# Keys and queries of the first three tiles loaded and transposed by 128 tokens, and the first masks added by TensorE

## The chip, the cores and the metric

The kernel runs on one core of one Trainium2 chip. The metric is device time in microseconds (us) of one execution, the median of several runs. The engines of a core work at the same time, each through its own queue in program order: TensorE (PE, with its weight loads shown apart as PEld), VectorE (DVE), ScalarE (ACT), GpSimd (POOL) and SyncE (SP). They wait for each other through semaphores. POOL, SP and ACT also issue DMA transfers.

## What is computed

Sliding-window attention with a window of 32 tokens to each side, over 8 batches and 8 heads of 576 tokens of 64 values, followed by a two-layer network with a sigmoid-approximated GELU over all 4,608 tokens:

```python
scores = scale * np.matmul(q, k.transpose(0, 1, 3, 2))
mask = np.abs(pos[:, None] - pos[None, :]) <= window     # 32
scores = np.where(mask, scores, -1000000000.0)
attn = softmax(scores)
x = concat_heads(np.matmul(attn, v))                     # 4608 x 512
h = x @ w_in                                             # 512 x 2048
out = (h * (1.0 / (1.0 + np.exp(-1.702 * h)))) @ w_out   # 2048 x 512
```

## The kernel before

All tokens are one row of 4,608, shifted by 32 so that a unit of 128 queries needs 192 keys: three chunks of 64. There are 36 units (u), nine tiles of 512 tokens (i or T, four units each), and halves of a tile of 256 tokens (t). The order of the work on every engine is written out by hand: the program's order is the order of each queue. `head` holds the first part (units 0 to 6 of attention, the two layers of units 0 to 3, and the first layer of units 4 to 7), `pairs` the next, and then `step` runs once for each T from 3 to 10.

The attention of a unit goes through these functions. `scores(u)` makes 24 matmuls, keys as weights and queries moving, into a pair of PSUM banks of the kind "d" (there are two such pairs), and ScalarE takes the exponential into `p`. `band(u)` multiplies `p` by a 0/1 mask on VectorE, in two halves or in one. `values(u)` makes 32 matmuls of `p` with the values and a column of ones: `ve` holds 128 tokens of v, `vo` the same shifted by 64 tokens, made by `odd_v` with two copies on VectorE or POOL. `norm(u)` divides on VectorE (a reciprocal and a product, or two of each), and `x_T(u)` transposes the result for the first layer, by TensorE and a copy, or by a DMA transpose on SP.

`layer1(t, d)` is a first-layer group: eight matmuls and a GELU on ScalarE. Each half tile has eight of them; d names a part of 256 columns of w_in. `layer2(u, part)` is a piece of two matmuls of the second layer; `run(n)` in `head` issues 2n of these. From tile 2 on the two layers use sums of quarter blocks (`first_layer`, `second_layer`, `x_sums`, `g_sums`). `keep_busy(n)` issues n matmuls on a tile of zeros.

Keys lie transposed in `kT` (two heads of 64 on the partitions), a ring of 1,024 tokens; queries in `qT`, two tiles. For tiles 0 to 2 `load_heads` (L144) loads several heads of a whole tile with four neighbouring tokens on a partition, so that a packet is 4 x 64 values. `heads_T` (L206) transposes them on TensorE, one head and every fourth token at a time (64 rows to a transpose), eight for each pair of heads; VectorE copies the keys to `kT`, putting the four token classes back in order, and ScalarE copies the queries as they are. Scores of units under 12 therefore have their query columns permuted, and the exponential writes `p` in order again (L269 to L271). The first pair of heads of tile 0 comes as float32 over SP (`load_first`) and is rounded by `pair_heads`, with four full transposes. The last 64 keys that unit 3 needs come apart (`load_edge`, `edge_T`). From tile 3 on keys and queries are loaded by 128 tokens of all heads (`load_keys`, `load_queries`), a packet being 64 values, and transposed by DMA (`keys_X`, `queries_X`) or by TensorE in four full transposes (`keys_PE`, L169).

All bfloat16 and float16 loads are issued by POOL, whose queue also holds the mask's making (`setup_mask`, `cut_mask`) and some of the `odd_v` copies. A POOL load waits for the one eight before it.

Of the kernel before, what the change touches and what calls it, by code (L numbers as in the profile page):

```python
# [22 lines left out]
SQ = 64  # L23
# [10 lines left out]
class _Kernel:  # L34

    def __init__(self, ctx, tc, q, k, v, w_in, w_out, out):
# [18 lines left out]
        self.stage, self.paired = {}, set()  # L55
# [51 lines left out]
    def setup_mask(self):  # L107

        pool, m = self.nc.gpsimd, self.mask
        lo, hi = slice(0, 64), slice(64, 128)  # L110
        pool.memset(m, 1.0)
        for blks, rows, sign in ((slice(0, 2), lo, 1), (slice(0, 2), hi, -1), (slice(2, 4), lo, -1), (slice(2, 4), hi, 1)):
            ap = m[rows, blks, :]
            pool.affine_select(out=ap, in_=ap, compare_op=ALU.is_ge, fill=0.0, base=0,
                               pattern=[[0, 2], [-sign, SQ]], channel_multiplier=sign)

    def cut_mask(self):
        lo, hi = slice(0, 64), slice(64, 128)
        for b, rows, cols in ((0, hi, slice(0, 32)), (0, lo, slice(32, 64)), (2, lo, slice(0, 32)), (2, hi, slice(32, 64))):
            self.nc.gpsimd.memset(self.mask[rows, b, cols], 0.0)  # L120
# [5 lines left out]
    def load_w_in(self, c):  # L126
        w = self.DFF // 4
        self.nc.gpsimd.dma_start(self.w_in_sb[:, :, c * w:(c + 1) * w],
                                 self.w_in[:, c * w:(c + 1) * w].rearrange("(k p) f -> p k f", p=128))
# [14 lines left out]
    def load_heads(self, i, c, heads=None):  # L144

        key = (c, i)
        if key not in self.stage:
            tag, bufs = ("qs", 2) if c == "q" else (("gs3", "gs1", "gs2")[i], 1)
            self.stage[key] = self.work.tile([128, self.H, JT * self.D], BF16, name=c + "s", tag=tag, bufs=bufs)
        lo, hi = heads or (0, self.H)  # L150
        src = {"q": self.q, "k": self.k}[c]
        for off, b, s, m in self.pieces(512 * i + (32 if c == "q" else 0), 512):
            self.nc.gpsimd.dma_start(self.stage[key][off // JT:(off + m) // JT, lo:hi, :],
                                     src[b, lo:hi, s:s + m, :].rearrange("h (p j) d -> p h (j d)", j=JT))
# [51 lines left out]
    def heads_T(self, c, i, hps, kind, eng):  # L206

        tp = self.bank(kind, [128, len(hps), JT, 128], BF16, "tp")
        for a, hp in enumerate(hps):
            for j in range(JT):  # L210
                if (c, i, hp) in self.paired:
                    self.nc.tensor.transpose(tp[:, a, j, :], self.stage[c, i, "c"][:, hp, j], self.ident)
                    continue
                for t in range(2):
                    self.nc.tensor.transpose(tp[64 * t:64 * t + 64, a, j, :],  # L215
                                             self.stage[c, i][:, 2 * hp + t, j * self.D:(j + 1) * self.D], self.ident)
        to = slice(hps[0], hps[-1] + 1)
        if c == "q":
            self.cast(eng, self.qT[:, to, i % 2], tp)
            return  # L220
        at = 512 * i % RING
        self.cast(eng, self.kT[:, to, at:at + 512].rearrange("r a (p j) -> r a p j", j=JT), tp.rearrange("r a j p -> r a p j"))

    def load_first(self, c, hp):

        raw = self.stage[c, "raw"] = self.work.tile([128, 2, JT * self.D], F32, name=c + "_raw", tag="s", bufs=3)
        src = {"q": self.q, "k": self.k}[c]
        s0 = 32 if c == "q" else 0
        self.nc.sync.dma_start(raw, src[0, 2 * hp:2 * hp + 2, s0:s0 + 512, :].rearrange("h (p j) d -> p h (j d)", j=JT))

    def pair_heads(self, c, i, hp, eng, src):

        st = self.stage[c, i, "c"] = self.work.tile([128, 1, JT, 2, self.D], BF16, name=c + "c", tag="x", bufs=5)
        self.paired.add((c, i, hp))
        self.cast(eng, st[:, hp], src.rearrange("p h (j d) -> p j h d", j=JT))

    def load_edge(self):

        self.stage["edge"] = self.work.tile([64, self.H, self.D], BF16, name="edge", tag="x", bufs=5)
        self.nc.gpsimd.dma_start(self.stage["edge"], self.k[0, :, 512:576, :].rearrange("h s d -> s h d"))  # L240

    def edge_T(self, kind, eng):
        nc = self.nc
        src = self.stage["edge"]
        tp = self.bank(kind, [128, 4, 64], BF16, "tp")
        for hp in range(4):
            nc.tensor.transpose(tp[:, hp, :], src[:, 2 * hp:2 * hp + 2, :], self.ident[:64, :64])
        self.cast(eng, self.kT[:, :, 512:576], tp)

    def scores(self, u):  # L250
        nc = self.nc
        both, two = self.double("sc")
        sc = [t.rearrange("p (b s) -> p b s", s=SQ) for t in two]
        if u < 12:
            qT = self.qT[:, :, u // 4 % 2].rearrange("r h j (b s) -> r h b j s", s=16)
            b0 = u % 4 * 2
        else:
            qT, b0 = self.qT[:, :, u // 4 % 2, u % 4].rearrange("r h (b s) -> r h b s", s=SQ), 0
        for hp in range(4):
            for chunk in range(3):  # L260
                lo, blks = 64 * (chunk % 2), slice(max(chunk - 1, 0), min(chunk, 1) + 1)
                at = 64 * (2 * u + chunk) % RING
                for eo in range(2):
                    r = slice(eo * 64, eo * 64 + 64)
                    nc.tensor.matmul(sc[eo][lo:lo + 64, 2 * hp + blks.start:2 * hp + blks.stop, :], self.kT[r, hp, at:at + 64],  # L265
                                     qT[r, hp, b0 + blks.start:b0 + blks.stop],
                                     start=hp == 0 and chunk < 2, stop=hp == 3 and chunk > 0)
        p = self.work.tile([128, 2, 8, SQ], BF16, name="p", tag="p", bufs=4)
        if u < 12:  # L269
            nc.scalar.activation(p.rearrange("p e b (r j) -> p (e b) r j", j=JT),  # L270
                                 both.rearrange("p e (b j r) -> p (e b) r j", j=JT, r=16), AF.Exp, scale=self.scale)  # L271
        else:
            nc.scalar.activation(p.rearrange("p e b s -> p e (b s)"), both, AF.Exp, scale=self.scale)  # L273
# [313 lines left out]
    def keep_busy(self, n):  # L587

        junk = self.bank("d", [128, 256], F32, "junk")
        for _ in range(n):  # L590
            self.nc.tensor.matmul(junk, self.idle[:, 0:128], self.idle, start=True, stop=True)  # L591


    def head(self):

        nc, dve, act, pool = self.nc, self.nc.vector, self.nc.scalar, self.nc.gpsimd
        for c in "kq":
            self.load_first(c, 0)
        self.setup()
        for h in ((2, 4), (4, 8)):  # L600
            for c in "kq":
                self.load_heads(0, c, h)
# [4 lines left out]
        self.load_edge()  # L607
        self.load_v(3)
        self.load_v(4, 0)
        self.load_w_in(0)  # L610
        self.odd_v(1, pool)
        self.load_w_in(1)
        self.load_w_in(2)
        self.odd_v(2, pool)
        self.odd_v(3, pool)
        self.load_w_in(3)
        self.cut_mask()
        for c in range(2):
            self.load_w_out(c)
        for c in "kq":  # L620
            self.load_heads(1, c)
        self.load_w_out(2)
        self.load_v(4, 1)
        for m in range(5, 8):
            self.load_v(m)
        self.load_w_out(3)
        for c in "kq":
# [324 lines left out]
```

## Time and profile before

| What | Value |
|---|---|
| median of 3 runs | 293.45 us (292.95 to 293.47) |
| profiled execution, whole | 292.87 us |
| its span, first instruction to last | 291.2 us |
| busy PE | 279.8 us, 96% |
| busy DVE, ACT, POOL | 69%, 69%, 43% |
| HBM read, written | 36.83 MB, 9.44 MB |
| packets under 512 bytes | 126,288 of 141,687 |

A row of the page's second part cuts the span into 40 equal slices of 7.3 us and gives a busy share in tenths. Tables by stretches give busy microseconds of each engine in a stretch, with the number of instructions in brackets. The chain of waits follows the work that ended last back from the last instruction: each step is the piece of work that released the next. In the rows of DMA queues, q0 is POOL's, q1 is SP's; a share over 100% means that several packets of an engine were under way at once. Matmul ends are modelled, so a busy TensorE is not one at its peak.

The page's groups that the change touches (line, engine, operation, shapes, count; busy us, mean ns):

| Group | Count | Busy us | Mean ns |
|---|---|---|---|
| L215 PE transposes of keys, 64 rows | 88 | 3.6 | 222 |
| L215 PE transposes of queries, 64 rows | 88 | 3.5 | 220 |
| L174 PE transposes of keys, 128 rows | 32 | 3.1 | 219 |
| L270 ACT exponential, units under 12 | 12 | 11.7 | 1,025 |
| L273 ACT exponential, other units | 24 | 23.3 | 1,031 |
| L286 DVE band, half | 14 | 5.3 | 420 by halves of 128x512 |
| L124 DVE copy of keys, 128x1024 from 64-row transposes | 4 | 4.9 | 1,224 |
| L124 ACT copy of queries, 128x1024 | 4 | 4.0 | 1,012 |
| L591 PE junk matmuls | 48 | 8.4 | 310 |

A matmul's own time includes the way through the array; neighbours follow each other faster than that.

### The profile page before, as it was taken

Reading aid. Unit: us, or ns where it says so; the run is one execution under the profiler, and the core shown is the slowest. Engines: PE = TensorE matmul, PEld = TensorE weight load, DVE = VectorE, ACT = ScalarE, POOL = GpSimd, SP = SyncE. Lnnn points to the kernel's source line nnn. Section 1 sums busy time; section 2 is a strip of 40 time slices with the busy share of each in tenths; the row PEclk is TensorE's granted clock in tenths of the full one; section 3 lists DMA queues with packets and bytes.
Section 4 is the critical chain, followed back from the end, with each engine's and each line's share of the span. In section 5 each row is a group of like instructions: output and inputs, shape, how many; then the busy total and the mean of one; then the engine's idle time right before and its main releaser. Section 6 shows DMA issues by size and latency. Waiting matters only on the chain.

```text
span 291.2 us, 8833 instructions
## 1 busy us (share of the span) xinstructions
PE 279.8 (96%) x3692; PEld 224.5 (77%) x3692; DVE 200.8 (69%) x404; ACT 201.6 (69%) x301; POOL 125.5 (43%) x191
## 2 busy tenths in 40 slices
PE   6789999999999999999899999999999999999995
PEld 4558855776866768888788888888888788888884
DVE  3467346887467579777867787778777877737752
ACT  3475625589795679768966897689758975756830
POOL 8894465839983398539326926802100000000000
PEclk9999999999999999999999999999999999999999
DMA  7999999999999999999999999999703120300223
GB/s 133 162 206 202 192 184 181 220 131 146 155 142 150 111 175 119 150 139 118 155 168 123 146 198 136 154 145 181 80 2 144 24 56 0 147 0 2 79 104 108
DMA packets 141687, 37.60 MB, mean 129 GB/s; under 512 B 126288, under 2 KB 137552, under 8 KB 141648
## 3 DMA queue, kind: packets, MB, share of 16 engines
q0 software_dynamic: 98528, 18.16, 86.2%
q1 hardware_dynamic: 41040, 15.35, 34.9%
q10 hardware_dynamic: 2080, 3.54, 4.8%
q8 instruction: 29, 0.48, 0.7%
q14 instruction: 10, 0.08, 0.1%
HBM read 36.83 MB, written 9.44 MB: 159 GB/s over the span
## 4 chain that ended last, share of the span: by engine, by line
PE 75%; ACT 15%; DVE 3%; issue 2%; DMA 2%; POOL 1%; POOLq 0%; ACTq 0%
PE h_ps L432 28%; PE o_ps L503 21%; PE h_ps L343 10%; PE o_ps L355 8%; ACT p L273 6%; PE pv L302 3%; ACT g L438 3%; ACT L273 2%; DMA ks<-in_k_dram 2%; PE tp L215 2%; ACT L585 2%; PE sc L265 1%; ACT h_ps L449 1%; DVE p L286 1%; PE junk L591 1%
## 5 line engine op out<-in xcount | busy, mean ns | idle before, releaser
L432 PEld LDWEIGHTS <-w_in_s 128*128 128x128 f16 x448 | 42.7, 97 | 10.7 <-issue 3.6
L438 ACT ACTIVATE g<-h_ps 128x512 f16<-128x512 f32 x49 | 29.2, 595 | 28.3 <-PE h_ps L432 26.6
L503 PEld LDWEIGHTS <-g 128*128 128x128 f16 x448 | 43.4, 98 | 5.2
L432 PEld LDWEIGHTS <-w_in_sb 128*128 128x128 f16 x336 | 32.5, 98 | 7.4 <-issue 0.6
L193 POOL DMA_DIRECT2D ve<-in_v_dram x40 | 33.7, 859 | 7.1 <-DMA w_out_sb<-in_moe_w_out_dram 4.0
L183 POOL DMA_DIRECT2D qu<-in_q_dram x30 | 24.1, 809 | 29.5 <-DMA qT<-qu 20.7
L503 PEld LDWEIGHTS <-gs 128*128 128x128 f16 x336 | 32.8, 98 | 4.2
L467 DVE TENSOR_TENSOR c<-h_ps,c 128x512 f32<-128x512 f32 x28 | 19.2, 687 | 22.3 <-PE h_ps L432 19.4
L203 POOL COPY vo<-ve 64x264 int32<-64x264 int32 x57 | 27.1, 475 | 17.1 <-DMA ve<-in_v_dram 9.4
L438 ACT ACTIVATE g<-c 128x1024 f16<-128x1024 f32 (+1 forms) x35 | 34.0, 970 | 0.0
L432 PE MATMUL h_ps<-xT,w_in_s 128*128 128x256 f16 x224 | 33.6, 272 | 0.0
L432 PE MATMUL h_ps<-xs,w_in_s 128*128 128x256 f16 x224 | 31.7, 272 | 1.4 <-issue 0.9
L432 PE MATMUL h_ps<-xT,w_in_sb 128*128 128x256 f16 x224 | 32.4, 272 | 0.3
L355 PE MATMUL o_ps<-w_out_sb,g 128*128 128x512 f16 x128 | 32.6, 380 | 0.0
L161 POOL DMA_DIRECT2D ks<-in_k_dram x27 | 22.8, 853 | 20.3 <-PE tp L174 9.7
L503 PE MATMUL o_ps<-w_out_s,g 128*128 128x256 f16 x224 | 31.5, 273 | 0.0
L343 PE MATMUL h_ps<-xT,w_in_sb 128*128 128x256 f16 x256 | 30.5, 273 | 0.0
L503 PE MATMUL o_ps<-w_out_s,gs 128*128 128x256 f16 x224 | 29.5, 272 | 0.0
L286 DVE TENSOR_TENSOR p<-p,mask 128x1024 bf16<-128x1024 bf16 (+1 forms) x43 | 24.8, 599 | 5.5 <-ACT p L270 3.3
L343 PEld LDWEIGHTS <-w_in_sb 128*128 128x128 f16 x256 | 24.2, 98 | 3.3 <-DVE xT L124 0.2
L503 PE MATMUL o_ps<-w_out_sb,g 128*128 128x256 f16 x224 | 26.6, 273 | 0.0
L345 ACT ACTIVATE g<-h_ps 128x512 f16<-128x512 f32 x32 | 18.9, 596 | 9.2 <-PE h_ps L343 9.1
(91 smaller groups left out, 468.7 us busy)
## 6 DMA issues: line engine op xcount, KB each, us to landing
ve<-in_v_dram POOLq DMA_DIRECT2D x32, 128.0 KB, 7.6
out_dram<-o_sb SPq DMA_DIRECT2D x6, 512.0 KB, 4.9
out_dram<-o_sb ACTq DMA_DIRECT2D x6, 512.0 KB, 6.8
ks<-in_k_dram POOLq DMA_DIRECT2D x23, 128.0 KB, 9.1
qu<-in_q_dram POOLq DMA_DIRECT2D x18, 128.0 KB, 8.9
out_dram<-o_sb SPq DMA_DIRECT2D x9, 256.0 KB, 4.6
w_in_sb<-in_moe_w_in_dram POOLq DMA_DIRECT2D x4, 512.0 KB, 7.4
w_out_sb<-in_moe_w_out_dram POOLq DMA_DIRECT2D x4, 512.0 KB, 11.3
```

What stands on the lines that cost most here:

```text
L161: self.nc.gpsimd.dma_start(ks[off:off + n], self.k[b, :, s:s + n, :].rearrange("h s d -> s h d"))
L183: self.nc.gpsimd.dma_start(qu[off:off + n], self.q[b, :, s:s + n, :].rearrange("h s d -> s h d"))
L193: self.nc.gpsimd.dma_start(self.ve[m % NV][off:off + n, :, :self.D], self.v[b, :, s:s + n, :].rearrange("h s d -> s h d"))
L203: eng.tensor_copy(to, src)
L273: nc.scalar.activation(p.rearrange("p e b s -> p e (b s)"), both, AF.Exp, scale=self.scale)
L286: self.nc.vector.tensor_mul(part, part, msk.to_broadcast([128, n, 2, SQ]))
L343: nc.tensor.matmul(hps[:, i, :], self.w_in_sb[:, kr, ff * 128:(ff + 1) * 128], xT[:, kr, :], start=(i == 0 and kr == 0), stop=(i == 1 and ...
L355: nc.tensor.matmul(o_ps, g[:, ff, s * 128:(s + 1) * 128], self.w_out_sb[:, ff, :], start=(ff == 0), stop=(ff == self.NFF - 1))
L432: nc.tensor.matmul(ps[:, i, :], a[:, kr, (2 * j + i) * 128:(2 * j + i + 1) * 128], x[:, kr, :], start=first and i == 0 and kr == 0, stop=i ...
L438: act.activation(out, src, AF.Gelu_apprx_sigmoid)
L467: dve.tensor_add(c22, ps, c22)
L503: nc.tensor.matmul(out, a[:, kb, p * 128:p * 128 + 128], b[:, kb, :], start=first and n in (0, 2 * two) and kb == 0, stop=n in (3, 3 - 2 * ...
```

## The change

Tiles 0 to 2 of keys and queries are loaded by `load_units` with 128 tokens of all eight heads on the partitions, a packet being 64 values, and `units_T` transposes them in four full transposes for each unit; `both_T` does two units of keys and queries in one pair of banks. `load_raw` brings the first unit of keys and all four units of queries of tile 0 as float32 over SP and ACT, and `round_raw` rounds them. The special case of units under 12 goes.

For units 0 to 3, `scores` first adds a negative mask (-30,000 outside the window) to both banks with two matmuls by the identity, so that the exponential gives zeros there, and `band` is not called. `negative_mask` makes it on VectorE. `setup_mask` makes only the two outer mask blocks, and `cut_mask` copies them.

The order in `head` is new: w_in is loaded in two eighths and three quarters, among the loads of v; `odd_v(1)` goes from POOL to VectorE; the table of the GELU is loaded before the first `layer1`; first-layer groups come in another order; seven rounds of the second layer come before the transposes of tile 1 instead of four. In `pairs`, `odd_v` of 10, 11 and 13 goes from POOL to VectorE.

```diff
+    def negative_mask(self):
+        self.neg = self.work.tile([128, 4, 2, SQ], BF16, name="neg", tag="x", bufs=5)
+        msk = self.mask[:, 1:4:2, :].rearrange("p (o b) s -> p o b s", o=1)
+        self.nc.vector.tensor_scalar(self.neg, msk.to_broadcast([128, 4, 2, SQ]), -1.0, 30000.0, op0=ALU.add, op1=ALU.mult)
...
+    def load_units(self, c, i, units, half=None):
...
+                    self.nc.gpsimd.dma_start(self.stage[c, i][off:off + m, u], src[b, :, s:s + m, :].rearrange("h s d -> s h d"))
...
+    def both_T(self, i, units, engs):
+        tp = self.bank("d", [128, 2, 2, 4, 128], BF16, "tp")
...
+    def transpose_units(self, c, i, units, tp, n=128):
+        for a, u in enumerate(units):
+            for hp in range(4):
+                self.nc.tensor.transpose(tp[:, a, hp, :], self.stage[c, i][:n, u, 2 * hp:2 * hp + 2, :], self.ident[:n, :n])
...
+    def load_raw(self, c, u, queue):
+        raw = self.stage[c, "raw", u] = self.work.tile([128, self.H, self.D], F32, name=c + "_raw", tag="s", bufs=3)
...
+        queue.dma_start(raw, src[0, :, s0:s0 + 128, :].rearrange("h s d -> s h d"))
...
-    def scores(self, u):
+    def scores(self, u, neg=None):
...
+        for eo in range(2 if neg is not None else 0):
+            nc.tensor.matmul(two[eo], self.ident, neg.rearrange("p h b s -> p (h b s)"), start=True, stop=False)
...
     def head(self):
...
+        self.load_raw("k", 0, nc.sync)
+        self.load_raw("q", 0, act)
+        self.load_units("q", 0, ())
+        self.load_units("k", 0, (1,))
+        self.load_raw("q", 1, nc.sync)
         self.setup()
+        self.load_units("k", 0, (2,))
         for m in range(2):
             self.load_v(m)
         self.setup_mask()
         self.load_v(2)
+        self.load_units("k", 0, (3,))
+        self.load_units("k", 1, (0,), 0)
+        self.load_w_in(0, 1)
         self.load_v(3)
+        self.load_w_in(1, 2)
         self.load_v(4, 0)
+        self.load_w_in(2, 4)
         self.odd_v(2, pool)
+        self.load_w_in(4, 6)
         self.odd_v(3, pool)
+        self.load_w_in(6, 8)
...
+        self.scores(0, self.neg)
+        self.units_T("k", 0, (2,), "o", dve)
         self.odd_v(0, dve)
+        self.round_raw("q", 3, dve)
+        self.keep_busy(4, "t")
+        self.scores(1, self.neg)
+        self.keep_busy(2, "h")
+        self.values(0, "ot")
+        self.odd_v(1, dve)
         self.norm(0)
+        self.units_T("q", 0, (2, 3), "d", act)
+        self.units_T("k", 0, (3,), "d", dve)
+        self.keep_busy(2, "h")
+        self.values(1, "hh")
         self.norm(1)
+        self.keep_busy(2, "o")
+        self.x_T(0, "o", act)
+        self.keep_busy(2, "t")
+        self.scores(2, self.neg)
+        self.units_T("k", 1, (0,), "t", dve, 64)
+        self.x_T(1, "h", dve)
+        self.keep_busy(4, "h")
+        self.scores(3, self.neg)
+        self.gelu_table()
         self.layer1(0, 0)
         self.values(2)
         self.norm(2)
         self.values(3)
         self.norm(3)
+        self.layer1(0, 1)
         self.x_T(2, "t")
         self.x_T(3, "o")
+        self.layer1(1, 0)
+        self.layer1(1, 1)
...
-        run(4)
+        run(7)
+        self.both_T(1, (0, 1), (dve, act))
+        run(1)
+        self.both_T(1, (2, 3), (dve, act))
...
+        self.load_v(8)
+        self.load_keys(3, (0,))
+        for m in (9, 10, 11, 12):
+            self.load_v(m)
         self.load_queries(3)
+        self.load_keys(3, (1, 2, 3))
...
     def pairs(self):
...
-        self.odd_v(10, pool)
...
         self.norm(8)
+        self.odd_v(10, dve)
         self.x_T(8)
...
-        self.odd_v(11, pool)
...
         self.band(10, 1)
+        self.odd_v(11, dve)
...
         self.x_T(11)
+        self.odd_v(13, dve)
```

## The prediction

> **What bounds the kernel now.** I read the page's busy rows first, then the busy time by stretches, then the chain of waits, then the opening's timeline.
>
> ```profile
> span 291.2 us, 8833 instructions
> PE   6789999999999999999899999999999999999995
> DMA  7999999999999999999999999999703120300223
> 0.00:24.00 24.00, 18.87 (x312) 13.12 (x313) 11.82 (x41) 12.17 (x16) 20.91 (x42) 1.00 1.30 170
> 24.00:64.00 40.00, 40.00 (x519) 28.19 (x520) 25.77 (x49) 22.39 (x31) 21.08 (x27) 1.00 1.70 190
> 64.00:92.00 28.00, 27.05 (x510) 18.94 (x500) 19.95 (x44) 22.88 (x33) 21.50 (x30) 1.00 1.89 144
> 92.00:291.00 199.00, 193.92 (x2373) 164.30 (x2371) 143.27 (x271) 144.17 (x224) 62.04 (x93) 1.00 1.09 110
> ```
>
> In the stretches the columns are the stretch, its length, busy PE, PEld, DVE, ACT and POOL, then granted clock, DMA share and GB/s. TensorE is idle for 5.1 us before 24, for nothing between 24 and 64, and for 1.0 between 64 and 92. So this change, which ends with the third tile, can gain in two ways only: the steady TensorE stream starts earlier, or TensorE gets less to do after it has started. The junk matmuls of L591 (8.4 us in all) count as busy in the first row, so the opening holds more air than 5.1 us.
>
> ```profile
> 3.07 5.78 DMA ks<-in_k_dram
> 8.89 0.64 PE tp L215 x16
> ...
> 10.78 1.08 ACT qT L124 x2
> 12.21 1.03 ACT p L270
> ...
> 22.14 0.98 PE h_ps L343 x8
> ...
> 24.45 10.48 PE h_ps L343 x96
> 34.92 3.45 PE o_ps L355 x16
> 38.38 1.01 PE tp L215 x32
> ```
>
> The chain (start, length, what) begins with the load of heads 4 to 7 of the keys, goes through their transposes to the first exponential at 12.21, and reaches the steady stream with the third first-layer group at about 22.1. All sixteen groups are done at 34.92. That is my milestone. A steady group costs 10.48/12 = 0.873 us.
>
> **The opening, step by step.** The old order needs all 512 tokens before any score; the new one needs 128 tokens of keys and queries, then 64 more keys. What comes late in the new order is the loads, so they are counted first.
>
> ```profile
> q1 hardware_dynamic: 479, 0.47, 90.6%
> q0 software_dynamic: 1245, 0.61, 112.8%
> q0 software_dynamic: 2973, 0.39, 237.2%
> q1 hardware_dynamic: 496, 0.13, 86.6%
> q0 software_dynamic: 437, 0.05, 85.9%
> ```
>
> These are the DMA rows (packets, MB, share of 16 engines) of four windows: 2.0 to 3.7, 4.0 to 8.5, 9.5 to 12.0, and 70.3 to 71.3 us (the last two lines). Packets of 1,024, 512 and 128 bytes flow at 282, 277 and 1,189 a us; the mix of 256-byte transposes and 128-byte rows at 933. Every load of 128 tokens is now 1,024 such short packets. In the new queue order ten of them come up to the third load of v: five float32 ones on the SP and ACT queues and five on POOL's. Ten times 1,024 take 8.6 us at 1,189 and 11.0 at 933. No row shows float32 packets of 256 bytes from DRAM; I take 1,090 (9.4 us), nearer the fast end, because the slow mix holds transposes, which these loads are not. First packets flow at 1.95 us, and landing follows the last packet by about 1.05 (the second v load's packets end near 11.1, its copy starts at 12.22). So the third v load lands at 12.4, bounds 11.6 and 14.0; in the old order it lands at 12.97.
>
> Everything before it fits: first keys at about 4.4, cast 0.56, four transposes 0.4, copy 0.42 (ACT's 0.59 for the queries, which ACT rounds in 0.62), first exponential near 8.5 instead of 12.21. The negative mask (one DVE instruction on 128x512, between 0.2 and 0.7 by the DVE rows of that size) stands between two key copies that wait for loads, so I put it at nothing; uncovered it costs those 0.2 to 0.7.
>
> From 12.4 on VectorE works in a row, in program order: `odd_v(1)` two copies of 0.29 (13.0); `norm(0)` two reciprocals of 0.17 and two products of 0.42 (14.2); copy of the keys' fourth unit 0.42 (14.6); `norm(1)` 1.2 (15.8). TensorE then does x_T(1) 0.22, four junk 0.44, and the scores of unit 3: two mask matmuls of 512 columns at 0.22 (L355's rate, 3.45/16) and 0.44 as before: 17.3. Exponential 1.03 (18.4), `values(3)` 0.4. The four `band` products, eight times 0.42 with the mask, are gone from this path. VectorE's `norm(2)` and `norm(3)`, 0.9 each, run from 18.55 to 20.35; copies of x for units 2 and 3, 0.42 each: 21.2. With 0.1 us of hand-overs layer1(1,0) starts at 21.3 to 21.4, two groups being done, as at 22.08 before. Fourteen groups of 0.873 are 12.2: **33.6 against 34.92, so -1.3 us**; bounds from the landing alone -2.1 and +0.3.
>
> POOL's part: `odd_v(2)` and `odd_v(3)` stay on it (two copies of about 0.42 each), and behind them the issue of the next w_in parts (0.76 each). v unit 3 now waits behind one w_in eighth, the half unit behind two. An eighth (512 packets of 512 bytes) takes 1.3 us at the rate of the window from 44 to 46 us (790 packets in 2 us), 1.9 at the opening's 277 a us. So they land near 15.9 and 17.7, `vo` of unit 3 is ready near 18.8, when `values(3)` is issued. That is without slack: a microsecond later there is a microsecond later at the milestone.
>
> The later key and query loads, 8 times 128 tokens for each of tiles 1 and 2, grow too: 2.1 MB at 154 instead of 190 GB/s, 13.6 instead of 11.0 us. Tile 1's second half then lands near 39.5 and is transposed at 41; tile 2's lands near 52 (before 50.15) and is used from 56. Cover 1.5 and 4 us, cost nothing; if the cover went, the excess of 2.6 would show.
>
> The Trainium skill's page "DMA: Bandwidth & Descriptors" (Specifications) gives 512 bytes as the smallest transfer for line rate. By that rule the change makes the wrong choice on every key and query load, and the trace agrees in direction, 154 against 190 GB/s. The rule alone gives no time; the sum above charges what the rows show.
>
> **TensorE after the opening.** Tiles 1 and 2: 64 matmul transposes of 64 rows each, 1.01 per 32 (chain), become 32 each of 128 rows; L174's and L332's fours follow each other in 0.22, so 16 cost 0.88. Four times (1.01 - 0.88) = **-0.5**. The layer-2 calls are only reordered, scores have the same count of matmuls, and the exponential without the rearranged write costs the same (1,025 against 1,031 ns).
>
> **The stage after (64 to 92).** `odd_v(10)` and `odd_v(11)` move from POOL to VectorE, before `band(10)` and before `band(11)`, two copies of 0.39 each. VectorE has little room there: `norm(9)` would end at 75.8 instead of 74.56, and `values(11)`, which reuses its bank pair at 75.03, waits 0.75. `odd_v(13)` falls into VectorE's idle 4.92 us before 81.38 and costs nothing. Bounds 0 (hidden by earlier loads or idle moments) and 1.5 (all of it); I take **+0.6**. POOL's relief buys nothing TensorE waits for.
>
> **Sum.** -1.3 - 0.5 + 0.6 = -1.2. The profiled execution took 292.87 us (span 291.2), so 291.67; the runs' median is 293.45, 0.58 above it, so **292.2**.
>
> **Rivals.**
> *More of the same*: short packets flow at 1,189 from the start, v lands at 11.6 (-0.8 more), and VectorE's added copies hide (-0.6): -2.6, 290.85. For: 1,189 is reached as soon as 128-byte packets start. Against: the queue share there is 237%, with several loads in flight, and TensorE's fixed order has little slack.
> *Given back*: v's half unit lands a microsecond later behind the eighths at 277 packets a us, so the milestone gains 0.3 to 0.4, and the added copies cost 0.9: about 0, 293.45.
> *Slower*: the float32 loads are the bound. In the window 65.75 to 66.15, where 256-byte packets ran alone, 234 passed in 0.4 us, 585 a us: a raw load is 1.75 us, five are 8.75, and with the POOL loads behind them v lands at 16.0; at the mixed 933 it lands at 14.0. The middle, 15.0, is 2.6 later than I took: +1.4, 294.85. It decides from a landing of 13.6 on. For: no float32 load with so short packets is in the trace, and five of ten loads are such. Against: those 585 were transposes.
> The skill's page "DMA: Bandwidth & Descriptors" (Issuing engines are not separate DMA queues) says that issuing on several engines saves only issue time. By it the raw loads on SP and ACT would take engine time from v, as in this rival; nothing in this trace shows two hardware queues at once at the start.
>
> **How the numbers follow.** Forecast 0.46, more 0.22, given back 0.12, slower 0.20. About 0.2% (0.6 us) is what a measurement of this kernel can tell. The forecast's own spread, half of the way to the bounds of the landing and of the copies together, is 291.5 to 293.4, so some 0.08 of its 0.46 is within 0.2%; faster is 0.38 + 0.22 = 0.60, same 0.08 + 0.12 = 0.20, slower 0.20. The range runs from 290.4 (beyond the second case) to 295.0 (the slower one's middle).
>
> **What would show it.** First exponential near 8.5; third v load at 12.4; layer1(1,0) at 21.4 and all sixteen groups at 33.6; transposes of tiles 1 and 2 in fours of 0.22 without waits for loads; a gap of up to 0.75 before `values(11)`. A first-layer stream that waits on `ks` or `ve` loads later than 13.6 would make the forecast wrong, and so would TensorE gaps between 34 and 64, where there were none.

## The result, and the profile after

The changed kernel takes 295.08 us (median of 4 runs, 294.73 to 295.46), against 293.29 of the kernel before (4 runs, 292.95 to 293.47). The ratio is 1.0063, with an interval of [1.0045, 1.008]: it is slower, by 0.6%, where a gain, to 292.2, was forecast. The profiled execution took 295.05, its span is 293.3.

The head of the page of the changed kernel, TensorE's and the DMA engines' rows in 40 slices:

```profile
span 293.3 us, 8654 instructions
...
PE   7888999898999999999999999999999999999995
...
DMA  9999999999999999999999999982303050300133
```

TensorE is fuller in the first two slices (78 for 67) than it was, but now has an 8 in the fourth, eighth and tenth, where it had nines. The busy time by stretches, with the columns of the same table before:

```profile
0.00:24.00 24.00, 19.43 (x278) 13.02 (x281) 11.26 (x43) 11.73 (x15) 19.18 (x39) 1.00 1.49 182
24.00:64.00 40.00, 39.19 (x426) 28.06 (x424) 22.56 (x44) 21.93 (x31) 30.92 (x38) 1.00 2.00 184
64.00:92.00 28.00, 25.94 (x494) 18.19 (x493) 20.12 (x47) 23.42 (x33) 17.46 (x23) 1.00 2.34 145
```

TensorE's idle time was 0 between 24 and 64 and is 0.81; between 64 and 92 it was 0.95 and is 2.06. Who is waited for is in the table of TensorE's waits from 24 to 92 us (total, times, longest):

```profile
PE pv L296 <- DVE x L309: 1.0, 2, 0.6
PE pv L296 <- DVE x L314: 0.7, 1, 0.7
PE tp L326 <- DVE x L309: 0.6, 1, 0.6
PE pv L296 <- DVE p L280: 0.3, 1, 0.3
PE pv L296 <- DVE vo L208: 0.2, 1, 0.2
```

Every one ends with VectorE (0.6 of the first row, at 91.96, and the 0.3 stand in the kernel before too). No wait of TensorE in these stages ends with a load. The chain of waits has the three steps that answer to the forecast's milestone (start, length, what):

```profile
19.05 0.98 PE h_ps L337 x8
...
23.22 12.40 PE h_ps L337 x112
35.62 6.04 PE o_ps L349 x28
```

The sixteen first-layer groups are done at 35.62; the forecast said 33.6, and before it was 34.92. Times of the same piece of work in the two traces:

| Piece of work | Before | Forecast | After |
|---|---|---|---|
| first exponential | 12.21 | 8.5 | 10.22 |
| third v load landed | 12.97 | 12.4 | 12.86 |
| `norm(1)` ends on VectorE | | 15.8 | 16.02 |
| layer1(0,0) starts | 18.59 | 17.3 | 18.98 |
| layer1(1,0) starts, two groups done | 22.08 | 21.4 | 23.22 |
| sixteen groups done, second layer (chain) | 34.92 | 33.6 | 35.62 |
| `keys_PE(3, 0)`, end of `head` | 63.43 | | 64.61 |
| first matmul of L432/L426, after `pairs` | 82.04 | | 84.61 |

The third v load and the end of `norm(1)` were forecast to within half a microsecond. The first exponential was not, and neither was TensorE's work behind `norm(1)`. VectorE's timeline shows that it was not the v load that it waited for:

```profile
10.75 0.43 DVE L131 CAST qs<-q_raw 128x512 bf16<-128x512 f32 x1 [2.67 <-DMA q_raw<-in_q_dram]
...
12.66 0.85 DVE L208 COPY vo<-ve 64x528 bf16<-64x528 bf16 x2
```

It waits for the float32 queries of unit 2, which land at 10.73, and then works without a gap to 16.02. The second of the two copies in the last line, the one that needs the third v load, starts at 13.09, 0.23 after that load has landed.

From 76 to 143 us the same matmuls run 2.57 later than before. Behind that each of the two profiles has a stop of its own. Before, TensorE stood for 0.88 us inside a group, with nothing that it waited for:

```profile
144.30 0.39 PE L432 MATMUL h_ps<-xs,w_in_s 128*128 128x256 f16 x2
145.57 0.27 PE L432 MATMUL h_ps<-xs,w_in_s 128*128 128x256 f16 x1 [0.88 <-issue]
```

The changed kernel stands for 0.79 us at the start of a `values`; the exponential that is named there had ended 0.48 us earlier:

```profile
146.92 0.19 PE L296 MATMUL pv<-ve,p 128*64 128x65 bf16 x1 [0.79 <-ACT p L267]
```

Behind both stops the matmuls are 2.35 apart, and the spans 2.1. Eight of the fourteen profiles have one such stop, of 0.58 to 0.88 us: five of them, all of the changed kernel and its variants, among the first matmuls of this same `values`, the others elsewhere. b1, a2, a3, a6 and c2 have none. So one profile's end can carry most of a microsecond that seems to belong to the run; the experiments are read by stretches first, and by their medians second.

### The profile page after: what moved, and what is told of

Same layout as the page of the kernel before. It is cut to its first block, busy times and chain, and to the rows that moved or that the text cites. A ratio compares the mean times of both kernels' runs of the same rounds, so it can differ in the third digit from the quotient of the medians.

```text
span 293.3 us, 8654 instructions
## 1 busy us (share of the span) xinstructions
PE 280.9 (96%) x3598; PEld 225.5 (77%) x3600; DVE 199.0 (68%) x409; ACT 201.6 (69%) x301; POOL 129.4 (44%) x193
## 4 chain that ended last, share of the span: by engine, by line
PE 70%; ACT 15%; DVE 7%; issue 3%; DMA 2%; POOL 2%; ACTq 0%; POOLq 0%
PE h_ps L426 28%; PE o_ps L497 20%; PE h_ps L337 8%; PE o_ps L349 7%; ACT p L267 6%; ACT g L432 3%; PE pv L296 2%; ACT L267 2%; DMA ks<-in_k_dram 2%; DVE p L280 2%; ACT L579 2%; DVE x L309 2%; PE tp L228 1%; DVE o_sb L131 1%; PE sc L263 1%
## 5 line engine op out<-in xcount | busy, mean ns | idle before, releaser
L426 PEld LDWEIGHTS <-w_in_s 128*128 128x128 f16 x448 | 42.7, 97 | 9.7 <-issue 2.6
L432 ACT ACTIVATE g<-h_ps 128x512 f16<-128x512 f32 x49 | 29.1, 595 | 28.4 <-PE h_ps L426 26.7
L267 ACT ACTIVATE p<-sc 128x1024 bf16<-128x1024 f32 x36 | 35.3, 1028 | 6.1 <-PE sc L263 5.3
L426 PEld LDWEIGHTS <-w_in_sb 128*128 128x128 f16 x336 | 32.6, 98 | 7.4 <-issue 0.6
L432 ACT ACTIVATE g<-c 128x1024 f16<-128x1024 f32 (+1 forms) x35 | 33.9, 970 | 0.0
L426 PE MATMUL h_ps<-xT,w_in_s 128*128 128x256 f16 x224 | 33.6, 272 | 0.0
L426 PE MATMUL h_ps<-xT,w_in_sb 128*128 128x256 f16 x224 | 32.4, 272 | 0.3
L208 POOL COPY vo<-ve 64x264 int32<-64x264 int32 x49 | 22.0, 449 | 24.0 <-PE pv L296 17.0
L426 PE MATMUL h_ps<-xs,w_in_s 128*128 128x256 f16 x224 | 31.6, 272 | 0.6
```

The source lines that it names most:

```text
L208: eng.tensor_copy(to, src)
L426: nc.tensor.matmul(ps[:, i, :], a[:, kr, (2 * j + i) * 128:(2 * j + i + 1) * 128], x[:, kr, :], start=first and i == 0 and kr == 0, stop=i ...
L432: act.activation(out, src, AF.Gelu_apprx_sigmoid)
```

## Experiments

Four stretches of each trace: start of the second layer; from there to `keys_PE(3, 0)` ("24 to 64"); from there to the first matmul of L426 (L432 before; "64 to 82"); and the next hundred matmuls of that line ("after 82").

| Kernel | Median us | Ratio to before, interval | Second layer starts | 24 to 64 | 64 to 82 | After 82 |
|---|---|---|---|---|---|---|
| before | 292.9 to 293.3 | | 34.76 | 28.67 | 18.61 | 23.63 |
| after | 295.08 | 1.0063 [1.0045, 1.008] | 35.45 | 29.16 | 20.00 | 23.64 |
| a1_banks | 295.35 | 1.0079 [1.0058, 1.01] | 35.73 | 29.00 | 19.90 | 23.85 |
| b1_parity | 293.75 | 1.0035 [1.0015, 1.0056] | 34.59 | 28.68 | 19.54 | 23.64 |
| a2_junk | 295.18 | 1.0071 [1.0046, 1.0096] | 35.05 | 28.92 | 20.00 | 24.09 |
| a3_odd | 295.25 | 1.0087 [1.006, 1.0114] | 35.75 | 29.60 | 19.76 | 23.98 |
| a5_nojunk | 296.14 | 1.0097 [1.006, 1.0135] | 34.35 | 28.80 | 20.33 | 26.70 |
| a6_l2 | 295.06 | 1.0068 [1.0045, 1.0091] | 35.48 | 28.35 | 19.99 | 24.99 |
| a4_warm | 296.20 | 1.0135 [1.0069, 1.0201] | 35.51 | 29.54 | 20.01 | 23.78 |
| a8_band | 301.01 | 1.0265 [1.0225, 1.0305] | 42.98 | 28.80 | 19.99 | 23.63 |
| c1_all | 293.68 | 1.0023 [1.0, 1.0046] | 34.37 | 28.38 | 19.08 | 25.67 |
| c2_late | 291.90 | 0.9967 [0.9947, 0.9987] | 34.01 | 28.31 | 18.87 | 23.64 |
| a9_late | 295.33 | 1.0084 [1.0056, 1.0112] | 35.45 | 28.81 | 20.00 | 24.38 |
| a7_noload | 294.78 | 1.0063 [1.0039, 1.0086] | 35.46 | 28.80 | 20.01 | 23.63 |

Most of the story is in this table: most of the single repairs shorten their own stretch, the time does not follow, and the last column says where much of it went.

### The bank that values(7) comes to: a1_banks and b1_parity

`bank("h")` hands out the banks h and i in turn. The opening of the kernel before asks it for "h" eight times (four transposes, `values(0)` twice, two `x_T`), the changed one five times (two, `values(1)` twice, one), so the number of calls ahead of `values(7, "hi")` is odd. Its "h" half then falls on bank i, the bank of its other half. a1 makes the call "hh", so that the halves fall on different banks again; b1 gives the kernel before the same fault.

```diff
-        self.values(7, "hi")
+        self.values(7, "hh")
```

```diff
+        self.turn ^= 1
         self.values(7, "hi")
```

> The changed kernel with values(7) asking for its two banks so that they always differ. Theory: in the changed kernel an odd number of calls has moved the alternating bank by one, so both halves of values(7) fall into one bank and the second waits for VectorE's division of the first (0.74 us of TensorE idle at 69.6, values(7) taking 1.31 instead of 0.38). Expected: values(7) back to 0.38, the layers' steady stream after it 0.9 us earlier, time about 294.2. Rival: that wait is covered by a later one (values(11), the exponentials of units 9 to 11), and the time stays at 295.1.

> The kernel before, with the alternating bank moved by one just ahead of values(7), nothing else. Theory: this alone brings the same wait: values(7) 1.3 instead of 0.38 us, time 0.9 us longer, about 294.2. Rival: the wait comes from VectorE's new copies in the changed kernel, and the kernel before stays at 293.3.

The timeline of TensorE in the changed kernel, at the second half of `values(7)`:

```profile
69.61 0.22 PE L296 MATMUL pv<-ve,p 128*64 128x65 bf16 x1 [0.74 <-DVE x L314]
```

and in b1, at the same call:

```profile
68.26 0.22 PE L302 MATMUL pv<-ve,p 128*64 128x65 bf16 x1 [0.74 <-DVE x L320]
```

The second half waits until VectorE has read the first half out of the bank, 0.74 us in both. b1's matmuls are 0.17 us ahead of those of before up to that call, and 0.77 behind them from there to 142 us: 0.94 for one change of parity. This is shown: the change moved a parity that no line of its text mentions. b1's median is 0.63 above that of before, where 0.9 was expected.

In a1 the wait is gone, yet the stretch is hardly shorter (19.90 for 20.00). Its timeline two microseconds later:

```profile
70.61 0.38 PE L263 MATMUL sc<-qT,kT 64*64 64x64 bf16 x18
...
71.73 0.25 PE L263 MATMUL sc<-qT,kT 64*64 64x64 bf16 x6 [0.74 <-issue]
```

Eighteen of the 24 matmuls of `scores(11)` run, then TensorE stands for 0.74 without a semaphore, as in the profile of before at 145.57. Why is open. Without this stop the stretch would be 19.16, 0.84 shorter, about the 0.9 that was expected; that is an estimate. The median did not gain either (295.35 for an expected 294.2), so a1 alone does not show a gain of time; c1 and c2, below, show one for it and three other repairs together.

### The junk in the opening: a2_junk and a5_nojunk

```diff
-        self.keep_busy(4, "h")
+        self.keep_busy(4, "o")
         self.scores(3, self.neg)
```

```diff
-        self.keep_busy(2, "t")
         self.scores(2, self.neg)
...
-        self.keep_busy(4, "h")
         self.scores(3, self.neg)
```

> The changed kernel with the four junk matmuls ahead of the scores of unit 3 written to another bank, which is free by then. Theory: the scores of unit 3 and the first first-layer group wait because these junk matmuls share a bank with the transposes of x of unit 1 and so wait for VectorE's copy of it (0.51 us idle at 17.65). Expected: scores of unit 3 0.6 us earlier, the end of the sixteen first-layer groups at 35.0 instead of 35.6, time about 294.5. Rival: the copies to kT or the landing of loads set the scores of unit 3 anyway, less than 0.2 us.

> Changed kernel without the two junk matmuls ahead of scores(2) and without the four ahead of scores(3); nothing else. Theory (the opening's loss is TensorE's own order: junk that shares a bank with x_T(1) and waits for its copy): 0.22 of two junk, 0.44 of four and the 0.51 us wait ahead of them go, so that the first first-layer group starts 1.0 to 1.2 us sooner after the end of norm(1) than in the changed kernel (there 16.02 to 18.98, so about 1.9 after norm(1) instead of 2.96), and the second-layer start comes 0.6 to 1.2 sooner; time 294.0 to 294.5. Rival (the opening hangs on late loads and VectorE): first-layer start moves by under 0.3, time as the changed kernel's, 295.1.

TensorE's timeline in the changed kernel, from the first transposes of x to the first group of the first layer:

```profile
15.19 0.38 PE L326 MATMUL tp<-ident,x 128*128 128x128 f16 x4
15.41 0.38 PE L585 MATMUL junk<-idle 128*128 128x256 bf16 x2
15.62 0.38 PE L254 MATMUL sc<-neg,ident 128*128 128x512 bf16 x1
16.15 0.44 PE L263 MATMUL sc<-qT,kT 64*64 64x64 bf16 x24
16.52 0.29 PE L228 MATMUL tp<-ident,ks 64*128 64x64 bf16 x4
16.74 0.40 PE L326 MATMUL tp<-ident,x 128*128 128x128 f16 x4
17.65 0.60 PE L585 MATMUL junk<-idle 128*128 128x256 bf16 x4 [0.51 <-DVE xT L131]
18.09 0.59 PE L254 MATMUL sc<-neg,ident 128*128 128x512 bf16 x2
18.61 0.44 PE L263 MATMUL sc<-qT,kT 64*64 64x64 bf16 x24
18.98 0.39 PE L337 MATMUL h_ps<-xT,w_in_sb 128*128 128x256 f16 x2
```

x of unit 1 is ready at 16.02, but its transposes stand in the program behind `scores(2)` and a key transpose and start at 16.74. Then the four junk matmuls write into the bank that these transposes have just filled, and wait until VectorE has copied it: work that is there to fill air makes 0.51 us of air, and runs 0.43 itself, ahead of the scores that the path needs. In a5:

```profile
16.75 0.40 PE L326 MATMUL tp<-ident,x 128*128 128x128 f16 x4
16.98 0.59 PE L254 MATMUL sc<-neg,ident 128*128 128x512 bf16 x2
17.51 0.44 PE L263 MATMUL sc<-qT,kT 64*64 64x64 bf16 x24
17.88 1.05 PE L337 MATMUL h_ps<-xT,w_in_sb 128*128 128x256 f16 x8
```

The first layer starts at 17.88 and the second at 34.35, both 1.10 sooner, although a5's loads landed about 0.25 later in that profile and `norm(1)` ended 0.64 later, at 16.66. The theory's stretch holds. a2, which only takes the bank away, gains 0.40 of it where 0.6 was expected; its median is 295.18, not 294.5. The time of a5, 296.14, is a miss for the theory: a5 is the slower kernel. Its "after 82" column is 3.06 longer, which the last group of experiments takes up.

### The second layer and the masks on VectorE: a6_l2

```diff
-        run(7)
+        run(6)
...
-        self.band(5)
         self.values(4)
         self.norm(4)
+        self.band(5)
...
         self.x_T(4, "d")
+        run(1)
         self.values(5)
```

> Changed kernel with one second-layer step moved from the opening of that stage to between x_T(4) and values(5), and with norm(4) ahead of band(5) on VectorE. Theory (x_T(4), x_T(5) and values(6) wait because VectorE's band work stands ahead of norm(4) and TensorE comes to them too early): the 0.58 wait at x_T(4) goes and the others stay or go, so that from the second-layer start to the third tile's first layer takes 18.5 to 18.8 us (changed 19.32, before 18.74); time 294.4 to 294.8. Rival (something later on VectorE sets this stretch, the wait moves to the next transposes or values): stretch 19.1 to 19.4, time 295.1.

The waits of TensorE from 24 to 64 us in a6 are one row, for x_T(5):

```profile
PE tp L326 <- DVE x L309: 0.3, 1, 0.3
```

The stretch is 28.35 instead of 29.16, and 0.32 below that of before; the 0.58 wait at x_T(4) is gone. In the other variants, whose code is the same here, the stretch varies from 28.80 to 29.60 with the wait of `values(6)` for `odd_v(6)` (0 to 0.61), so 0.45 is the part that the edit surely takes. The time, 295.06, did not move (294.4 to 294.8 was expected).

### The odd copies: a3_odd

```diff
+        self.odd_v(10, pool)
...
-        self.odd_v(10, dve)
...
+        self.odd_v(11, pool)
...
-        self.odd_v(11, dve)
```

> The changed kernel with odd_v(10) and odd_v(11) on POOL again, at their old places. Theory: on VectorE they delay norm(9), whose banks values(11) needs (0.38 us idle at 77.6). Expected: values(11) 0.4 us earlier, time about 294.7. Rival: POOL makes the shifted values too late (it issues loads there), and values(10) or values(11) wait longer: 295.1 or more.

In the changed kernel `values(11)` stands for 0.38 at 77.60, because `norm(9)` is late on VectorE; in a3 it does not. Against before, a3's matmuls fall 0.94 us back between 64 and 79 us, those of the changed kernel 1.39: the two copies cost 0.45 in place of the 0.6 of the forecast. The rest, 0.94, is `values(7)`. The median, 295.25, shows nothing of it; a3's profile had its loads 0.3 later and a 0.61 wait at `values(6)`.

### The clock and the masks: a4_warm and a8_band

```diff
-        self.keep_busy(14)
+        self.keep_busy(18)
```

> Changed kernel with 18 instead of 14 junk matmuls ahead of the first transposes, so that TensorE has no empty stretch of 0.79 us before the first keys land. Theory (that stretch costs the clock: matmuls run at half rate until 9.63 us): full rate from about 4.3 us, first exponential 0.5 to 0.8 sooner (9.5), but the first-layer start, which comes after the third value tile's landing at 12.9, moves by under 0.2; time 295.0. Rival (the half rate is carried through to the end): first-layer start 0.5 to 0.8 sooner, time 294.3 to 294.6. Second rival (the clock's window runs free): half rate for the first microseconds all the same.

In the changed kernel TensorE stands for 0.79 us before the first keys are rounded, and its four transposes at 5.09 take 0.40 from the first to the next instruction; later ones take 0.22. The granted clock of the page's rows is full there, so it is the spacing that tells. In a4 the same transposes take 0.23 from the start, and the first exponential comes at 9.24. This does not show that the gap is the cause. a9, whose opening is that of the changed kernel, has a gap of 0.94 there, and yet the same transposes in 0.24 and its first exponential at 9.18; a2, a5 and a7 have the full rate there too, and lose it from 7.5 to 7.8 until 10.9 to 11.2. The first layer starts at 19.04 in a4 and at 18.97 in a9 (18.98): what is won earlier is waited away until the raw queries of unit 2 land and VectorE's row starts (11.00 in a4, 10.75 in the changed kernel). The half rate costs next to nothing here, as the theory said; why some runs have it is open. The median of 296.20 rests on 4 runs from 295.19 to 299.47 and stays unexplained; its span is 293.5 against 293.3 of the changed kernel.

a8 takes the added masks out (`negative_mask`, and `self.neg` in the scores of units 0 to 3) and multiplies by the mask on VectorE again, each `band(u)` ahead of the `values(u)` that reads it:

```diff
-        self.scores(1, self.neg)
+        self.band(0)
+        self.scores(1)
```

> Changed kernel with the masks of units 0 to 3 multiplied by VectorE again (band) instead of added by TensorE. Theory (the added masks are worth something in the opening): eight 128x512 matmuls go from TensorE (0.22 each at full rate, about 2.0 with the half rate at the start), four multiplications of 0.68 come to VectorE, which is the opening's chain ahead of norm(1): second-layer start 0.7 to 2.0 later than in the changed kernel, time 295.8 to 297. Rival (TensorE's mask matmuls are what delays the opening): second-layer start 0.4 to 0.8 sooner, time 294.3 to 294.7.

It costs 7.5 us at the second layer's start, far over the 2.0 of the theory. The busy time by stretches of a8 shows why (the last three numbers are granted clock, DMA share, GB/s):

```profile
12.00:15.00 3.00, 1.83 (x48) 1.36 (x49) 2.84 (x10) 1.02 (x1) 2.10 (x3) 1.00 1.99 173
15.00:18.00 3.00, 1.61 (x26) 1.06 (x24) 2.45 (x8) 1.01 (x1) 1.50 (x3) 0.72 1.63 191
18.00:30.00 12.00, 9.97 (x124) 6.74 (x122) 4.67 (x14) 5.10 (x7) 7.87 (x16) 0.50 1.25 202
```

With the masks VectorE works for 2.45 of the 3 us from 15 to 18 (1.67 in the changed kernel; from 12 to 15 both are full), TensorE is busy for little more than half of 12 to 18 us, and then its granted clock is 0.50 up to 30 us, 13.7 us in all. The masks by TensorE are thus worth more than their own time: they keep VectorE's chain short and TensorE occupied. In the changed kernel TensorE is busy for 4.86 of the same 6 us and keeps 1.00. By the medians a8 is 5.9 us slower.

The Trainium skill says of the clock ("TensorE: Matmul & The Clock Gate", Part 1) that it falls after an idle window of about 3.4 us and rises after a busy one. Here it fell with no idle time of TensorE longer than 1.32 us before it, so by the measurement no idle window is needed. Idle time over any few microseconds does not decide either: c1 is busy for 2.40 of the 4 us from 88 to 92 and keeps 1.00, while a5, below, is busy for 2.34 of the same 4 us and does not. In each trace the changes of the granted clock lie whole multiples of 3.41 us apart (16.33 and 29.98 in a8, 93.13 and 96.54 in a5). In the fourteen traces, cut into such stretches, the clock fell behind the five in which TensorE was busy for 1.63 us (a8), 1.81 (a5) and 1.61 to 1.65 (at the start of a2, a5 and a7), and behind none that began at 1.00 with 1.98 or more.

### Where the gains went: c1_all, c2_late, a9_late, a7_noload

c1 has the edits of a1, a3, a5 and a6 at once. c2 is c1 with the five loads of tile 4's queries issued later; a9 is the changed kernel with that move alone:

```diff
-        self.load_queries(4)
         self.band(10, 1)
...
         self.load_keys(4, (1, 2, 3))
+        self.load_queries(4)
         self.load_keys(5, (0,))
```

a7 leaves out the loads of tile 2's keys and queries, and uses tile 1's in their place.

```diff
-        for u in range(4):
-            for c in "kq":
-                self.load_units(c, 2, (u,))
+        for c in "kq":
+            self.stage[c, 2] = self.stage[c, 1]
```

> Changed kernel with four waits taken out at once: no junk matmuls ahead of scores(2) and scores(3), the second-layer step and norm(4) moved as in the run before, values(7) with both halves in the two h banks, odd v copies 10 and 11 on POOL. Theory 'floor' (the loads of 128 tokens at a time leave the DMA engines behind, so that the last DMA transpose of tile 2's x lands at 86.3 to 87.4 us however early it is issued, 78.8 to 80.6 so far): the first x sum on VectorE stands near 86.5 to 87.5 with a wait of 2 to 3 us ahead of it, TensorE waits there too, and the time is 294.5 to 296 (more if the wait lets TensorE's clock fall). Rival 'sum of the waits': 295.1 less 1.1, 0.7, 0.7 and 0.4 = 292.2, no wait at the x sums.

> As the one before, and the five loads of tile 4's queries, which now stand ahead of the transposes of x in the DMA engines, are issued behind the loads of tile 4's keys. Theory 'floor': these five are 0.5 MB, 3.2 us at 154 GB/s; the last transpose of x lands near 83 to 84, the x sums follow without a wait or with one below 0.7, and the time is 292.0 to 293.0. Rival (the transposes are slow by themselves, 6 us from issue to landing): they land as late as ever, 86.3 to 87.4, time 294.5 to 296.

> Changed kernel with tile 4's query loads issued late, and nothing else. Theory: the last transpose of x lands 2 to 3 us sooner (83.5 to 84.5 instead of 86.45), but the x sums stand at 86.6 as before, since the masks ahead of them on VectorE end at 86.7: in the changed kernel its waits and the late transposes fall together, and taking one away gives nothing; time 295.1. Rival (the transposes alone hold the stage): time 292.5 to 293.5.

> Changed kernel without the loads of tile 2's keys and queries (eight of 128 tokens, 0.98 MB): tile 2 takes tile 1's staged rows instead, so its output is not the reference's. Theory: the DMA engines win 6 us by 55 us; the transposes of x take 4 to 5 us from issue instead of 6.3 and land by 84.5; the waits on VectorE and on bank i stay, so the time moves by under 0.5 (294.6 to 295.2). Rival (loads have held TensorE or VectorE between 24 and 80 us all along): 292.5 to 294.

In c1 the matmuls at 79 us stand 0.57 ahead of before, where the changed kernel's stand 2.57 behind: the four repairs are worth 3.1 us together. By 90 us c1 has lost 2.4 of it. A stop inside `scores` at 84.06, without a semaphore and like those above, is 0.62 of that. For the rest, VectorE's timeline in c1 at the first sums over tile 2's x:

```profile
82.87 0.69 DVE L280 TENSOR_TENSOR p<-p,mask 128x1024 bf16<-128x1024 bf16 x1 [0.22 <-ACT p L267]
85.86 0.43 DVE L373 TENSOR_TENSOR xs<-xT 128x512 f16<-128x512 f16 x1 [2.30 <-DMA xT<-x]
```

They wait for the DMA transpose of `x_T(11)`. The view of that line (L322), in c1:

```profile
  DVE xs L373: 2.3, 1
...
DMA to landing us min/median/max: 7.7/8.2/8.4
```

and in the changed kernel:

```profile
DMA to landing us min/median/max: 5.4/6.0/6.3
```

The changed kernel issues this transpose at 80.17 and it lands at 86.45; VectorE has just ended its masks at 86.7 and does not wait. c1 issues it at 77.58, and it lands at 85.77. In the traces from a1 to a6 it is issued between 78.78 and 80.62 and lands between 86.34 and 87.37, whoever is early. (Before, with the faults of b1: issued 77.95, landed 81.82.) So much of what is won ahead of 80 us is waited away here, unless the transposes land sooner too. c1's time, 293.68, lies between the two that were expected (294.5 to 296, and 292.2): neither theory held as it stood. c2 does that; its L373 has no wait:

```profile
82.59 0.69 DVE L280 TENSOR_TENSOR p<-p,mask 128x1024 bf16<-128x1024 bf16 x1 [0.22 <-ACT p L267]
83.20 0.42 DVE L373 TENSOR_TENSOR xs<-xT 128x512 f16<-128x512 f16 x1
```

The last transpose is issued at 77.05 and lands at 82.27, sooner than the 83 to 84 expected. The time is 291.9, 1.78 below c1's: the ratio, 0.9967 [0.9947, 0.9987], is below that of both kernels. That the query loads in front held the transposes is shown, for c1.

The wider theory, that loads of 128 tokens leave the DMA engines behind, fell. a7 leaves out 1.05 MB of them, and its last transpose still takes 5.9 us (79.83 to 85.74, over the 84.5 expected), with a time of 294.78, as expected. In a9 it lands at 86.92 where 83.5 to 84.5 was expected: there the moved loads are issued at 81.16, right behind the transpose of 80.66, and share the engines with it. What does fit all traces is that the transposes are slow while other loads are in flight; that was not tried by itself. In the changed kernel the late transpose (86.45) and the late masks on VectorE (86.7) fall together, so taking away one of them can give little: a7 moved the transpose by 0.7 and the ratio to before not at all (1.0063); c1 moved TensorE alone by 3.1, and lost 2.4 of it here, 0.62 by its stop.

The wait bears on a5's miss too. In its profile, which is that of the slowest of its six runs (297.15), VectorE waits 1.66 for the transpose, TensorE, 1.1 ahead at 84 us, waits behind it, and then, in the busy time by stretches:

```profile
88.00:92.00 4.00, 2.34 (x28) 1.40 (x27) 3.90 (x9) 2.08 (x5) 0.00 (x0) 1.00 1.77 162
92.00:96.00 4.00, 3.69 (x35) 2.52 (x36) 2.79 (x7) 0.49 (x2) 0.88 (x1) 0.64 0.62 94
```

TensorE is busy for 2.34 of 4 us, and its granted clock in the next stretch is 0.64, then 0.93: (1 - 0.64) times 4 and (1 - 0.93) times 4 are 1.7 us of work lost. That is the profiled run. Four of the six runs have a mean clock of 0.994 or more (0.987 in the profiled one) and still took 295.19 to 296.60, so the clock is not all of it; what makes the median 1.1 longer than that of the changed kernel is open in part.

## Why the prediction was wrong

**What bounds the kernel: right for TensorE's stream, by luck for the opening.** The third v load landed at 12.86 for 12.4, and `norm(1)` ended at 16.02 for 15.8. But VectorE's row did not start with that load: it ran without a gap from 10.75, when the raw queries of unit 2 had come, and reached the copy that needs v 0.23 after its landing. The *slower* rival (float32 loads the bound, deciding from a v landing of 13.6) did not happen in its terms, though a float32 load did start that row; its time, 294.85, is near the measured one for another reason. The half unit of v, for which the forecast saw no slack at 17.7, was waited for until 18.21 by POOL's copy, and no wait of TensorE ends with it.

**The opening, -1.3: wrong, it was +0.7. The failed step** is "TensorE then does x_T(1) 0.22, four junk 0.44, and the scores of unit 3 ...: 17.3". It let TensorE be free at 15.8. The runs showed in its place that x_T(1) stands behind `scores(2)` with its mask matmuls (+0.94, of which 0.22 is the later end of `norm(1)`), and that the junk shares bank h with it and waits for the copy (+0.69 up to the junk). 17.3 became 18.98. a5 gives 1.10 of this back; x_T(1) ahead of `scores(2)` was not tried. The step from there to layer1(1,0) was 4.1 and measured 4.24; the fourteen groups were 12.2 and measured 12.40.

**Half rate at the start: not foreseen, and nearly free** (a4, a9). The first exponential came at 10.22 for 8.5; about 1.0 of that is the half rate (9.24 and 9.18 without it), and it is covered by VectorE's wait for the raw queries. The other 0.7 stands behind the keys of unit 1, which the forecast's list to 8.5 does not name: their transposes wait for the load until 7.21 in a4.

**Transposes of tiles 1 and 2, -0.5: right in itself, sixteen take 0.89.** What failed is the clause "the layer-2 calls are only reordered". They were the cover of VectorE's masks and norms; with them in front, x_T(4), x_T(5) and `values(6)` wait, and the stretch grew by 0.49 (by 0.13 in the variants whose `values(6)` does not wait). a6 brings it to 0.32 below before.

**The stage after, +0.6: right in kind, too small.** The odd copies cost 0.45 (a3). The other 0.94 is the bank of `values(7)`, which the forecast didn't look for (a1, b1).

**Key and query loads of tiles 1 and 2 at nothing: right for the changed kernel.** No wait of TensorE ends with one; a run left out those of tile 2 only (a7). The rule of 512 bytes, quoted there from the Trainium skill's page "DMA: Bandwidth & Descriptors", did not decide the time: a7 moves 1.05 MB less in short packets, and its ratio to before is that of the changed kernel, 1.0063. The later transposes of x, which no line of the forecast named, are where loads did come to matter.

**The sum.** Forecast -1.2; the terms measured are +0.69, +0.49 and +1.39, 2.57 in the trace. What it left out is what the new order broke. With the four waits and the query loads mended, c2 stands 0.85 ahead of before from 79 us on (-0.75, -0.36 and +0.26 by stretches, for the -1.3, -0.5 and +0.6 of the forecast), and its median is 1.1 below. That does not make the change itself worth 1.1: c2 puts the odd copies back on POOL and moves `band(5)` and tile 4's query loads, which the change had left alone, and none of these repairs was tried on the kernel before.

## What to carry to other kernels

When a diff changes an order written by hand, list for each engine what stands ahead of the needed instruction, and for each bank who used it last, filler included; a call that hands out banks in turn carries its parity into stages that the diff does not touch. A stage that shows no waits has its cover from the order of its work, so a move "at no cost" has to name that cover. Before mending a wait, look for the next transfer or engine that the faster stream will meet: here four repairs worth 3.1 us brought 1.2 (by the ratios) to 1.4 (by the medians) until five loads were moved out of the way of a transpose.

## What the runs showed of the hardware that was not expected

- TensorE at half rate at the start in some profiles and not in others with the same opening (four transposes in 0.40 at 5.09 in the changed kernel, in 0.24 at 5.24 in a9), where the granted clock in the profile's rows is 1.00 in both.
- The granted clock fell to 0.50 for 13.7 us in a8 and for 3.41 us in a5, with no gap over 1.32 and 1.00 us. It fell behind stretches of 3.41 us, counted on from an earlier change of the clock, with TensorE busy for 1.81 us or less (53%), and in no trace behind one that began at 1.00 with 1.98 (58%) or more.
- TensorE stops inside a group of matmuls, with no semaphore: 0.88 (before, 145.57), 0.74 (a1, 71.73), 0.62 (c1, 84.06), 0.79 (a5, 149.07). Which kernel has one, and where, changes from profile to profile, and the cause is open.
- The last three of the four DMA transposes of tile 2's x take 4.6 to 5.2 us from issue to landing in c2 and 7.7 to 8.4 in c1.
